# An attention-and-scan kernel: two score tiles of three PSUM banks, each of which may lend its third bank to VectorE

## The chip, the cores and the metric

The kernel runs on one core of a Trainium2 chip. The metric is the device time of one execution in microseconds (us). Four compute engines matter here: TensorE (PE in the profile; PEld is its weight load), VectorE (DVE), ScalarE (ACT) and GpSimd (POOL); SP issues most DMAs. PSUM, where TensorE puts its results, is used as eight banks of 128 partitions x 512 float32.

## The reference

Two independent halves are computed from separate inputs and laid side by side in the output. Half A is a diagonal state-space layer over 2048 steps and 640 channels; half B is attention with 32 query heads of 20 numbers, one shared key and one shared value head, without a mask:

```python
# A: Bu = x @ B_bar.T (complex);  h[t] = Lam_bar * h[t-1] + Bu[t];  y = 2*Re(h @ C.T) + x*Dskip
# B:
q = (x @ wq).reshape(B, S, 32, 20).transpose(0, 2, 1, 3)
k = x @ wk
v = x @ wv
scores = einsum("bhqd,bkd->bhqk", q, k) * (20 ** -0.5)
o = einsum("bhqk,bkd->bhqd", softmax(scores), v)
out_B = o.transpose(0, 2, 1, 3).reshape(B, S, 640) @ wo
out = concatenate([y, out_B], axis=-1)          # (1, 2048, 1280), bfloat16
```

## The kernel before

**Attention.** The 32 heads and 2048 queries make 32 groups `g`: a block of 512 queries by four heads. A group has 64 *units*, one for each of four heads `j` and 16 blocks `kc` of 128 keys. A unit is one matmul of scores (keys by queries, 128x512, one PSUM bank), an exponential, and the multiplication of the exponential with the values, which adds into the bank `PV`. There are 2048 units in all. The four heads lie in four 32-row strips of the array, so that up to four units are multiplied by one *fill* (`fill_op`), a burst of matmuls that TensorE works off side by side.

**Two ways to an exponential.** Most units take ACT: `ex_op` (line 1263) reads a whole *score tile* from PSUM, `R[0]` or `R[1]` in turn, and writes bfloat16 exponentials to `P`. The others, called *D units* here, take DVE: `dx_op` (line 1269) reads one bank and makes an integer whose bits are an approximate power of two, and three cheap shifted copies (`sh_op`, line 1274) are made from it in SBUF; four matmuls with the values then take the place of one, so that the errors average out. `raw_op` (line 1307) copies a finished group out of `PV`.

**PSUM before.** `R[0]` has three banks, `R[1]` has two (`TILES = (3, 2)`), `PV` has one and `B` has two (`BANKS = 2`). A bank of `B` is taken, used and given back, either by one D unit or by a piece of background work; `owner` says who has it. `R[0]` may *lend* its third bank, keyed `R0c`, to a D unit: the fill is then two banks for ACT and one for DVE (`size, d, x = 2, True, 2`).

**Background work** runs in threads beside the attention: `sa` (the inputs of the scan: five matmuls into a bank, then the product of line 901), `su` and `sr` (POOL's products around the scan, whose lines are 917 and 928), `sy` (half A's output, line 962), `qt`/`qd_block` (queries of the next block), `proj` (the output projection of half B, line 1061), `norm` and `dense` (the division by the softmax's denominators). Each matmul chain of `sa`, `sy`, `qt` or `proj` locks one bank with its first matmul and frees it with the DVE instruction that reads the result.

**The order of everything** is found while the program is built. `main` keeps a clock for each engine and, at each step, collects the candidates (a fill, an exponential, a shift, a group of PV matmuls, the head of each thread), gives each the time at which it could begin plus a bias, and emits the earliest. `want_d` decides whether a fill takes a D unit along: not if DVE's backlog is over a threshold, not if no bank is free soon enough (`spared`), and not if a background thread has waited too long for a bank (`starved`). The thresholds are drawn at random by `vary`; `SEEDS` holds one seed for each of 64 stretches of the 2048 units. `pv_op` takes exponentials from `items`, `P` is a ring of ten tiles (`PTILES`), 25 units in all, and an exponential waits while its tile's last content is still unread (`tile_left`). The end is `last_ops`: the projection of the last query block, in banks of `R`, `B` and `PV` (lines 1094 to 1104).

Of the kernel before, what the change touches and what calls it, by code (L numbers as in the profile page):

```python
# [217 lines left out]
def act_t(n):  # L218
    return n / 1200.0 + 0.05
# [24 lines left out]
class _Kernel:  # L244
    S, D, H, DH = 2048, 640, 32, 20
    NC, NQB, NKC, NGG = 5, 4, 16, 8
    BANKS = 2
    PIECES = "abcd"
    TILES, PTILES, DUNITS, DSHIFT, QRING = (3, 2), 10, 9, 3, 4
    SHIFTS = (0, 33, 65, 95)  # L250

# [13 lines left out]
    SEEDS = (19006, 20002, 21006, 22006, 23001, 24003, 25001, 26002, 27008, 28003, 0, 30006, 31008, 32005, 33006,  # L265
# [28 lines left out]
    def alloc(self):  # L294
        S, NC = self.S, self.NC
        nc = self.nc
        self.R = [self.scope.enter_context(nc.psum_tensor(f"R{i}", [128, 512 * n], FP32))
                  for i, n in enumerate(self.TILES)]
        self.PV = self.scope.enter_context(nc.psum_tensor("PV", [128, 512], FP32))
        self.BB = self.scope.enter_context(nc.psum_tensor("B", [128, 512 * self.BANKS], FP32))  # L300
        self.B = [self.BB[:, 512 * i:512 * i + 512] for i in range(self.BANKS)] + [self.R[0][:, 1024:1536]]
        self.bkeys = [f"B{i}" for i in range(self.BANKS)] + ["R0c"]
        self.p.psum.update(["R0", "R0c", "R1", "R1b", "PV", *(f"B{i}" for i in range(self.BANKS))])
# [25 lines left out]
        self.sb("P", [128, self.PTILES * 5 // 2, 512], BF16)  # L329
# [7 lines left out]
        self.wq_raw = self.P[:].rearrange("p s n -> p (s n)")[:, 18 * 512:18 * 512 + NC * 640].rearrange("p (c n) -> p c n", c=NC)  # L337
# [92 lines left out]
    def setup(self):  # L430
# [51 lines left out]
        pk = ["P7", "P8", "P9"]  # L482
# [23 lines left out]
        banks = [(K.R[1], 0, "R1"), (K.R[1], 512, "R1b"), (K.BB, 0, "B0"), (K.BB, 512, "B1")]  # L506
# [39 lines left out]
        for m, src, keys in ((0, K.R[1][:, 0:1024], ["R1", "R1b"]), (1, K.BB[:, 0:1024], ["B0", "B1"])):  # L546
# [342 lines left out]
    def scan_in(self, ops, dve, b, c):  # L889
        K, NC, prog = self, self.NC, self.prog  # L890
        u = NC * b + c
        xs = [f"xaT{b % 2}_{i}" for i in range(NC)]
        gate = lambda: prog["u"] >= u and prog["x"] >= b
        for k, (nm, BT) in enumerate((("BTre", K.BTre), ("BTim", K.BTim))):
            h = Hold()
            for cd in range(NC):
                ops.append(self.mms([self.m1(lambda h=h: h.T[:, :], BT[:, cd, 128 * c:128 * c + 128],
                                             K.xaT[:, b % 2, cd, :], cd == 0, cd == NC - 1)],
                                    [f"{nm}{i}" for i in range(NC)] + xs, [None], accum=cd > 0, lock=cd == 0,
                                    gate=gate if cd == 0 else None, hold=h))  # L900
            dve(lambda e, k=k, h=h: e.tensor_tensor(  # L901
                K.tm[:, 2 * k:2 * k + 2, :], bass.AP(tensor=K.BB, offset=512 * int(h.key[1]),
                                                       ap=[[512 * self.BANKS, 128], [0, 2], [1, 512]]),
                K.cs[:, c, :, :], ALU.mult), [None, "cosT", "sinT"], [f"tm{2 * k}", f"tm{2 * k + 1}"], 1024, hold=h,
                free=True, done=(lambda: prog.update(a=u + 1)) if k else None)
# [162 lines left out]
    def last_ops(self, gates, normed):  # L1068

        K, NC = self, self.NC  # L1070
        spots = [(K.R[0], 0, 0, 512, self.TILES[0]), (K.R[1], 1, 0, 512, self.TILES[1]), (K.BB, 2, 0, 512, self.BANKS)]
        keys = [["R0"], ["R1"], ["B0", "B1"], ["R0c", "PV"]]
# [40 lines left out]
    def vary(self, seed):  # L1113

        r = self.rng = random.Random(seed)
        self.backlog = r.choice((2.5, 3.0, 3.5, 4.0, 5.0))
        self.spared = r.choice(((0.02, 0.02, 0.02), (0.05, 0.15, 0.02), (0.1, 0.3, 0.02), (0.02, 0.3, 0.02)))
        self.after = r.choice((0.1, 0.15, 0.2)), r.choice((0.35, 0.4, 0.5))
        self.few, self.wait, self.noise = r.choice((1, 1, 2)), r.choice((0.15, 0.25, 0.35)), r.choice((0.0, 0.05, 0.1))

        self.starved = dict(sy=r.choice((0.0, 1.0, 4.0, 99.0)), sa=r.choice((2.0, 99.0)),
                            proj=r.choice((0.0, 1.0, 4.0, 99.0)),
                            qt=r.choice((0.0, 1.0, 4.0, 99.0)))
        self.lend = r.choice((0.5, 1.0))
        self.open, self.first = r.choice((0.6, 0.7)), r.choice(("sy", "proj", None))

    def main(self):
# [10 lines left out]
        tile_left = {}  # L1138
# [27 lines left out]
        fins = self.last_ops([lambda: done(0), lambda: done(1), lambda: done() and cur["raw"] == NG and not (any(owner[:2]) or sy or norm or proj),  # L1166
# [3 lines left out]
        owner = ["rest", "rest", None]  # L1170
        rest[-1].done = lambda: owner.__setitem__(slice(0, 2), [None, None])
        holds, since = {}, {}
# [57 lines left out]
        def want_d(g, t, n_tile, lent=False):  # L1230
# [9 lines left out]
            if any(owner[:2]) and any(t - x > self.starved[name] * (name != "qt" or len(self.qsent) > 0) for name, x in since.items()):  # L1240
                return False
            return (backlog(t) <= self.backlog - 0.5 * n_tile
                    and p.begin("pe", (), (f"B{bank(None)}",)) <= t + self.spared[n_tile])

        def fill_op(n, out, d, x):
            lst, reads, writes = [], set(), ([f"R{n % 2}"] if out else []) + ["R0c"] * (len(out) == 3)
# [13 lines left out]
        def ex_op(n, size):  # L1260
            b = 5 * (n // 2 % (self.PTILES // 2)) + 3 * (n % 2)
            dst = K.P[:, b:b + size, :].rearrange("p a n -> p (a n)")
            return Op("act", lambda e: e.activation(dst, K.R[n % 2][:, 0:512 * size], ACT.Exp, scale=self.exp_scale),  # L1263
                      [f"R{n % 2}"] + ["R0c"] * (size == 3), [f"P{n % self.PTILES}"], occ=act_t(512 * size), lat=0.17)
# [20 lines left out]
        def pv_op(g):  # L1285
            lst, keys = [], set()
            for j in range(4):
# [3 lines left out]
                if how == "act":  # L1291
                    rhs, w = K.P[:, b, :], 0
                    keys |= {f"P{a}", "VP0"}
# [18 lines left out]
        while True:  # L1312
# [33 lines left out]
            full = bool(tiles) and tile_left.get(tiles[0][0] - self.PTILES, 0) > 0  # L1346
            if tiles:
                n, out = tiles[0]
                if tile_left.get(n - self.PTILES, 0) == 0:
                    offer("ex", ex_op(n, len(out)), 0.0)  # L1350
# [19 lines left out]
            for name, th in threads:  # L1370
# [50 lines left out]
            if kind == "bg":  # L1421
                th = dict(threads)[name]
                th.popleft()
                if o.lock:
                    owner[int(o.hold.key[1])] = name
                    since.pop(name, None)
                if o.free:
# [3 lines left out]
            elif kind == "fill":  # L1431
                out, d, x = arg
                self.units += len(out) + (d is not None)
                if out:
                    n = cur["fill"]
                    cur["fill"] += 1
                    tile_left[n] = len(out)
# [12 lines left out]
            elif kind == "ex":  # L1450
                n, out = tiles.popleft()
                cur["act"] += 1
                b = 5 * (n // 2 % (self.PTILES // 2)) + 3 * (n % 2)
                for i, (g, j, kc) in enumerate(out):
                    items[g][j].append(("act", kc, n % self.PTILES, b + i, n))
# [17 lines left out]
            elif kind == "pv":  # L1473
                g = cur["pv"]
                for j in range(4):
                    if items[g][j]:
# [3 lines left out]
                        if how == "act":  # L1480
                            tile_left[h] -= 1
# [49 lines left out]
```

## Time and profile before

| | |
|---|---|
| time, median of 3 runs | 770.23 us (769.33 to 770.93) |
| the profiled execution | 770.28 us, of which the span of the trace is 768.6 us |
| busy: ACT / DVE / PE / POOL | 752.5 / 708.3 / 704.8 / 446.0 us |
| exponentials on ACT | 677 instructions: 258 of three banks, 419 of two (1612 units) |
| D units on DVE | 436: 363 through `B`, 73 through the lent bank of `R[0]` |
| granted TensorE clock, mean | 0.989 |

In the profile's groups a row gives the line, the engine, the operation, the tiles (output <- inputs, with buffer numbers left out, so `R` is either score tile), the shapes, the count, and behind the bar the time during which at least one such instruction ran and the mean duration in ns; behind the second bar stands the engine's idle time before them, and who ended it. Matmuls overlap one another, and so do ACT's instructions: their spacing is shorter than their duration. All matmuls bear one line, 421, of the helper that emits them.

### The profile page before, as it was taken

To read this page: it belongs to the slowest core of one execution; us is meant where nothing else is said; L and a number is where in the kernel's file an instruction comes from. 1 tells how busy PE (TensorE), PEld (TensorE's weight loads), DVE (VectorE), ACT (ScalarE), POOL (GpSimd) and SP (SyncE) were. 2 spreads that over 40 slices of the span, in tenths; PEclk is the share of its full clock that TensorE was granted. 3 is DMA by queue.
4 is the path that set the end of the run, shared out by engine and by line. 5 is a ranking of instruction groups with operands and counts; after the bars stand their busy time and mean duration, and the time that the engine had idled before them with its cause. 6 is when DMAs were issued, how large, how long until landed. Compare 5 with 4: busy or idle time off the path is not lost.

```text
span 768.6 us, 16664 instructions
## 1 busy us (share of the span) xinstructions
PE 704.8 (92%) x6538; PEld 213.4 (28%) x6538; DVE 708.3 (92%) x1236; ACT 752.5 (98%) x710; POOL 446.0 (58%) x867
## 2 busy tenths in 40 slices
PE   5799988888889999998889999988889999889998
PEld 2222222222222333322223323322223332223333
DVE  5599999999998999999997999999999789999986
ACT  8999999999999999999999999999999999999995
POOL 5612354579989931088997300199986469990040
PEclk9899999899999999999999999999999999999999
DMA  9366301000021100220002100040000201000020
GB/s 186 57 143 134 74 16 49 8 24 14 3 51 30 42 8 27 56 60 15 15 9 67 42 23 9 23 93 10 15 15 28 66 33 34 14 15 17 18 61 35
DMA packets 61179, 31.50 MB, mean 41 GB/s; under 512 B 41510, under 2 KB 61102, under 8 KB 61102
## 3 DMA queue, kind: packets, MB, share of 16 engines
q1 hardware_dynamic: 59606, 30.14, 15.9%
q8 instruction: 52, 0.85, 0.5%
q10 hardware_dynamic: 1496, 0.30, 0.2%
q14 instruction: 25, 0.20, 0.1%
HBM read 9.21 MB, written 12.69 MB: 28 GB/s over the span
## 4 chain that ended last, share of the span: by engine, by line
ACT 74%; PE 15%; DVE 9%; POOL 1%; DMA 1%; issue 1%; ACTq 0%; DVEq 0%; POOLq 0%
ACT P L1263 72%; PE R L421 5%; PE PV L421 5%; PE B L421 4%; DVE Pd L1274 4%; DVE Pd L1269 3%; DVE hh L928 1%; DVE tm L901 1%; POOL tm L858 1%; DMA WO<-in_B_wk_dram 1%; ACT cs L691 1%; ACT Pd L690 0%; ACT KT L538 0%; DVE CGre L860 0%; ACT L503 0%
## 5 line engine op out<-in xcount | busy, mean ns | idle before, releaser
L1263 ACT ACTIVATE P<-R 128x1024 bf16<-128x1024 f32 (+1 forms) x677 | 733.1, 1354 | 4.3 <-PE R L421 1.8
L421 PE MATMUL R<-QT,KT 32*128 32x512 bf16 (+1 forms) x1685 | 266.9, 389 | 48.6 <-ACT P L1263 37.1
L1269 DVE TENSOR_SCALAR Pd<-B 128x512 int16<-128x512 f32 x363 | 245.5, 682 | 19.4 <-PE B L421 17.0
L1274 DVE TENSOR_SCALAR Pd<-Pd 128x1536 int16<-128x1536 int16 (+2 forms) x513 | 260.2, 541 | 0.4
L421 PE MATMUL PV<-Pd,VP 128*32 128x512 bf16 x1744 | 256.9, 386 | 2.0 <-DVE OTr L1307 1.0
L421 PE MATMUL PV<-P,VP 128*32 128x512 bf16 x1612 | 253.3, 389 | 0.7 <-DVE OTr L1307 0.6
L917 POOL TENSOR_TENSOR tm<-hh,cs 128x128 bf16<-128x128 f32 x320 | 163.9, 533 | 17.7 <-DVE hh L928 8.3
L421 PEld LDWEIGHTS R<-QT,KT 32*128 32x128 bf16 (+1 forms) x1685 | 66.1, 91 | 301.0 <-ACT P L1263 271.0
L421 PE MATMUL B<-QT,KT 32*128 32x512 bf16 x363 | 141.0, 389 | 0.0
L917 POOL TENSOR_TENSOR uh<-tm 128x128 bf16<-128x128 bf16 x160 | 81.0, 527 | 97.6 <-DVE tm L901 93.7
L917 POOL TENSOR_TENSOR W<-tm 128x128 bf16<-128x128 bf16 x160 | 93.5, 608 | 49.4 <-PE B L421 45.3
L421 PEld LDWEIGHTS PV<-Pd,VP 128*32 128x32 bf16 x1744 | 60.1, 94 | 65.7 <-issue 40.5
L421 PEld LDWEIGHTS PV<-P,VP 128*32 128x32 bf16 x1612 | 58.1, 94 | 58.8 <-issue 46.6
L1011 POOL TENSOR_TENSOR OTd<-OTd,rwide 128x128 bf16<-128x128 bf16 x80 | 33.2, 443 | 60.0 <-DMA OTd<-o_rows 58.2
L1269 DVE TENSOR_SCALAR Pd<-R 128x512 int16<-128x512 f32 x73 | 49.9, 683 | 3.0 <-PE R L421 2.4
L901 DVE TENSOR_TENSOR tm<-B,cs 128x1024 bf16<-128x1024 f32 x40 | 48.5, 1213 | 1.0 <-PE B L421 0.6
L858 POOL TENSOR_SCALAR tm<-W,sc 128x128 f32<-128x128 bf16 x40 | 32.3, 821 | 27.5 <-DVE CGre L860 15.9
L421 PE MATMUL B<-CGre,W 128*128 128x384 bf16 (+1 forms) x160 | 46.4, 305 | 0.0
L421 PE MATMUL B<-CGim,W 128*128 128x384 bf16 (+1 forms) x160 | 45.5, 299 | 0.0
L928 DVE TENSOR_TENSOR_SCAN hh<-sc,hini,uh 128x512 f32<-128x512 f32 x30 | 40.7, 1358 | 0.0
L421 PEld LDWEIGHTS B<-QT,KT 32*128 32x128 bf16 x363 | 32.9, 91 | 0.0
L421 PE MATMUL B<-xaT,BTre 128*128 128x512 bf16 x100 | 30.1, 384 | 0.1
(149 smaller groups left out, 437.2 us busy)
## 6 DMA issues: line engine op xcount, KB each, us to landing
o_rows<-OTr SPq DMA_DIRECT2D x32, 128.0 KB, 1.7
QT<-q_rows SPq DMA_DIRECT2D x30, 128.0 KB, 2.2
q_rows<-Qd SPq DMA_DIRECT2D x16, 160.0 KB, 2.9
OTd<-o_rows SPq DMA_DIRECT2D x16, 160.0 KB, 3.4
out_dram<-ystage SPq DMA_DIRECT2D x16, 160.0 KB, 1.9
out_dram<-ostage SPq DMA_DIRECT2D x12, 160.0 KB, 1.8
P<-in_B_wq_dram SPq DMA_DIRECT2D x1, 800.0 KB, 5.6
WO<-in_B_wo_dram SPq DMA_DIRECT2D x4, 200.0 KB, 3.4
```

Of the source, the lines that this page charges most:

```text
L421: ins = e.matmul(o() if callable(o) else o, lhsT=l, rhs=r, start=st, stop=sp, skip_group_check=True, **kw)
L691: act(lambda e, c=c, b=b: e.activation(K.cs[:, c, :, :].rearrange("p i n -> p (i n)"), K.tri[:, 4 * b + 2:4 * b + 4, :].rearrange("p r n - ...
L858: pool(lambda e, y=y, c=c, gy=gy, i=i: e.tensor_scalar(K.ctmp[:, i:i + 128], y[:, i:i + 128], sc[:, gy, c:c + 1], None, op0=ALU.mult), key ...
L901: dve(lambda e, k=k, h=h: e.tensor_tensor(K.tm[:, 2 * k:2 * k + 2, :], bass.AP(tensor=K.BB, offset=512 * int(h.key[1]), ap=[[512 * self.BA ...
L917: put(lambda e, c0=c0, end=end: e.tensor_tensor(out[:, c0:end], a[:, c0:end], b[:, c0:end], op), reads, [writes + h], n, gate=None if i el ...
L928: dve(lambda e, ri=ri, ini=ini: e.tensor_tensor_scan(K.hh[:, ri, :], dec, K.uh[:, ri, :], ini, ALU.mult, ALU.add), ["sc", *(f"uh{ri}{h}" f ...
L1011: ops.append(Op("pool", lambda e, c=c, m=m: e.tensor_tensor(K.OTd[:, m, c], K.OTd[:, m, c], K.rwide[:, c], ALU.mult), rw + [f"OTe{dd}" for ...
L1263: return Op("act", lambda e: e.activation(dst, K.R[n % 2][:, 0:512 * size], ACT.Exp, scale=self.exp_scale), [f"R{n % 2}"] + ["R0c"] * (siz ...
L1269: return Op("dve", lambda e: e.tensor_scalar(K.Pd[:, 0, u, :], K.B[x][:, :], self.d_off, 0.0, op0=ALU.add, op1=ALU.max), [key], [f"Pd{u}_0 ...
L1274: return Op("dve", lambda e: e.tensor_scalar(K.Pd[:, i, a:b, :], K.Pd[:, 0, a:b, :], float(self.SHIFTS[i]), 0.0, op0=ALU.subtract, op1=ALU ...
```

## The change

`R[1]` gets a third bank, taken from `B`, which keeps one. Either tile may lend its third bank. The PSUM tensor `R1` now spans four banks: the tile's three and then the one that is left, `B0`. Background chains and D units of the old kind share `B0` alone; `bank()` returns 0 or nothing. The tile of a fill is two wide while its third bank is owned by a D unit, whether that is of this fill or of an earlier one.

`P` is a ring of 25 single units in place of ten tiles. An exponential is put where the last one ended, or at 0 where it would not fit, and waits until each of its slots has been read (`pleft`, `vacant`).

`vary` draws more: `lend` may also be 0.0 (how much less backlog a lent bank asks for), `prefer` lets a lent bank go ahead of `B0`, and `gap` holds a thread's next chain back for 0, 4 or 8 us after its last. The 64 seeds are new. In the setup, the banks that hold the keys' projection are renamed, and so are the last projection's.

The diff, cut to its core:

```diff
-    BANKS = 2
-    TILES, PTILES, DUNITS, DSHIFT, QRING = (3, 2), 10, 9, 3, 4
+    TILE, PUNITS, DUNITS, DSHIFT, QRING = 3, 25, 9, 3, 4
+    PWQ = 18
...
-    SEEDS = (19006, 20002, 21006, 22006, 23001, 24003, ...
+    SEEDS = (14003, 0, 16003, 17002, 18007, 19002, 20006, ...
...
-        self.B = [self.BB[:, 512 * i:512 * i + 512] for i in range(self.BANKS)] + [self.R[0][:, 1024:1536]]
-        self.bkeys = [f"B{i}" for i in range(self.BANKS)] + ["R0c"]
+        self.RB = self.scope.enter_context(nc.psum_tensor("R1", [128, 512 * (self.TILE + 1)], FP32))
+        self.R = [self.R0, self.RB[:, 0:512 * self.TILE]]
+        self.B = [self.RB[:, 1536:2048], self.R[0][:, 1024:1536], self.R[1][:, 1024:1536]]
+        self.bkeys = ["B0", "R0c", "R1c"]
...
-        self.lend = r.choice((0.5, 1.0))
+        self.lend, self.prefer = r.choice((0.0, 0.5, 1.0)), r.choice((False, True))
+        self.gap = dict(sy=r.choice((0.0, 4.0, 8.0)), proj=r.choice((0.0, 4.0, 8.0)), sa=r.choice((0.0, 0.0, 4.0)),
+                        qt=r.choice((0.0, 0.0, 4.0)))
...
+        def slot(size):
+            return room[0] if room[0] + size <= self.PUNITS else 0
+
+        def vacant(size):
+            b = slot(size)
+            return not any(pleft[b:b + size]) and not (rest and b + size > self.PWQ)
...
-            f = [i for i in range(2) if owner[i] is None]
-            if not f:
-                return None
-            return min(f, key=lambda i: p.begin("pe", (), (f"B{i}",)))
+            return 0 if owner[0] is None else None
...
             if lent:
-                return (self.lend < 9 and owner[2] is None and t_left() and backlog(t) <= self.backlog - 0.5 * n_tile - self.lend
-                        and p.begin("pe", (), ("R0c",)) <= t + self.spared[n_tile])
+                return (owner[lent] is None and t_left() and backlog(t) <= self.backlog - 0.5 * n_tile - self.lend
+                        and p.begin("pe", (), (self.bkeys[lent],)) <= t + self.spared[n_tile])
...
-                    size, x = self.TILES[n % 2] - (n % 2 == 0 and owner[2] is not None), bank(None)
+                    lent = 1 + n % 2
+                    size, x = self.TILE - (owner[lent] is not None), bank(None)
                     d = want_d(g, t, n % 2)
-                    if not d and size == 3 and want_d(g, t, 0, True):
-                        size, d, x = 2, True, 2
+                    if (not d or self.prefer) and size == 3 and want_d(g, t, 0, lent):
+                        size, d, x = 2, True, lent
...
+                    if o.lock and t_left() and not (name == "qt" and not self.qsent):
+                        bias += max(0.0, last.get(name, -99.0) + self.gap.get(name, 0.0) - p.clock["pe"])
```

More of the change, by code (lines that the diff above doesn't have):

```diff
@@ L296, in alloc @@
         nc = self.nc
-        self.R = [self.scope.enter_context(nc.psum_tensor(f"R{i}", [128, 512 * n], FP32))
-                  for i, n in enumerate(self.TILES)]
+        self.R0 = self.scope.enter_context(nc.psum_tensor("R0", [128, 512 * self.TILE], FP32))
         self.PV = self.scope.enter_context(nc.psum_tensor("PV", [128, 512], FP32))
-        self.BB = self.scope.enter_context(nc.psum_tensor("B", [128, 512 * self.BANKS], FP32))
-        self.B = [self.BB[:, 512 * i:512 * i + 512] for i in range(self.BANKS)] + [self.R[0][:, 1024:1536]]
-        self.bkeys = [f"B{i}" for i in range(self.BANKS)] + ["R0c"]
-        self.p.psum.update(["R0", "R0c", "R1", "R1b", "PV", *(f"B{i}" for i in range(self.BANKS))])
+        self.RB = self.scope.enter_context(nc.psum_tensor("R1", [128, 512 * (self.TILE + 1)], FP32))
+        self.R = [self.R0, self.RB[:, 0:512 * self.TILE]]
+        self.B = [self.RB[:, 1536:2048], self.R[0][:, 1024:1536], self.R[1][:, 1024:1536]]
+        self.bkeys = ["B0", "R0c", "R1c"]
+        self.p.psum.update(["R0", "R0c", "R1", "R1b", "R1c", "PV", "B0"])
         self.sb("xbT", [128, NC, S], BF16)
@@ L328, in alloc @@
         self.sb("ident", [128, 128], BF16)
-        self.sb("P", [128, self.PTILES * 5 // 2, 512], BF16)
+        self.sb("P", [128, self.PUNITS, 512], BF16)
         self.sb("Pd", [128, 4, self.DUNITS, 512], I16)
@@ L481, in setup @@
                 ["wk_raw", "wk4"], ["wk4"], n=100)
-        pk = ["P7", "P8", "P9"]
+        pk = [f"P{u}" for u in range(self.PWQ, self.PUNITS)]
         go(self.dma(K.wq_raw, t["wq"].rearrange("(c p) n -> p c n", p=128), "wq", writes=["wq_raw"] + pk, kb=800))
@@ L503, in setup @@
         act(lambda e: e.activation(K.half[:, 2:3], K.half_pi[:], ACT.Exp), ["half_pi", "half"], ["half2"], n=1)
-        banks = [(K.R[1], 0, "R1"), (K.R[1], 512, "R1b"), (K.BB, 0, "B0"), (K.BB, 512, "B1")]
+        banks = [(K.RB, 0, "R1"), (K.RB, 512, "R1b"), (K.RB, 1024, "R1c"), (K.RB, 1536, "B0")]
         for bt, off, key in banks:
@@ L544, in copy @@
                         occ=dve_t(512))
-        for m, src, keys in ((0, K.R[1][:, 0:1024], ["R1", "R1b"]), (1, K.BB[:, 0:1024], ["B0", "B1"])):
+        for m, src, keys in ((0, K.RB[:, 0:1024], ["R1", "R1b"]), (1, K.RB[:, 1024:2048], ["R1c", "B0"])):
             dve(lambda e, m=m, src=src: e.tensor_reduce(
@@ L1070, in last_ops @@
         K, NC = self, self.NC
-        spots = [(K.R[0], 0, 0, 512, self.TILES[0]), (K.R[1], 1, 0, 512, self.TILES[1]), (K.BB, 2, 0, 512, self.BANKS)]
-        keys = [["R0"], ["R1"], ["B0", "B1"], ["R0c", "PV"]]
+        spots = [(K.R0, 0, 0, 512, 3), (K.RB, 1, 0, 512, 4), (K.RB, 2, 1024, 1536, 4)]
+        keys = [["R0"], ["R1"], ["R1c", "B0"], ["R0c", "PV"]]
         banks = [[T[:, a:a + 320], T[:, b:b + 320]] for T, _, a, b, _ in spots] + [[K.R[0][:, 1024:1344], K.PV[:, 0:320]]]
@@ L1137, in main @@
         begun = [[False] * 4 for _ in range(NG)]
-        tile_left = {}
         dunit_left = {}
@@ L1165, in main @@
         done = lambda k=None: all(x == 64 for x in taken) and not any(k in (None, n % 2) for n, _ in tiles)
-        fins = self.last_ops([lambda: done(0), lambda: done(1), lambda: done() and cur["raw"] == NG and not (any(owner[:2]) or sy or norm or proj),
+        fins = self.last_ops([lambda: done(0), lambda: done(1), lambda: done() and cur["raw"] == NG and not (any(owner) or sy or norm or proj),
                               lambda: done() and cur["raw"] == NG],
@@ L1169, in main @@
         threads = [("rest", rest), ("norm", norm), ("dense", dense), ("proj", proj), ("qt", qt), ("qr", qr), ("sy", sy), ("sa", sa), ("su", su), ("sr", sr), ("sc", sc_), ("sx", sx), *fins]
-        owner = ["rest", "rest", None]
-        rest[-1].done = lambda: owner.__setitem__(slice(0, 2), [None, None])
-        holds, since = {}, {}
+        owner = ["rest", None, "rest"]
+        rest[-1].done = lambda: owner.__setitem__(slice(0, 3, 2), [None, None])
+        pleft, room = [0] * self.PUNITS, [0]
+        def slot(size):
[3 more added lines that the diff above has]
+            return not any(pleft[b:b + size]) and not (rest and b + size > self.PWQ)
+        holds, since, last = {}, {}, {}
         def bank(o):
-            f = [i for i in range(2) if owner[i] is None]
-            if not f:
-                return None
-            return min(f, key=lambda i: p.begin("pe", (), (f"B{i}",)))
+            return 0 if owner[0] is None else None
         def made(g, j):
@@ L1228, in t_left, with want_d @@
             return taken[NG - 1] < 40
-        def want_d(g, t, n_tile, lent=False):
+        def want_d(g, t, n_tile, lent=0):
             if not (g > 0 or taken[g] >= 24) or d_group(g) is None:
@@ L1235, in want_d @@
             if lent:
-                return (self.lend < 9 and owner[2] is None and t_left() and backlog(t) <= self.backlog - 0.5 * n_tile - self.lend
-                        and p.begin("pe", (), ("R0c",)) <= t + self.spared[n_tile])
+                return (owner[lent] is None and t_left() and backlog(t) <= self.backlog - 0.5 * n_tile - self.lend
+                        and p.begin("pe", (), (self.bkeys[lent],)) <= t + self.spared[n_tile])
             if bank(None) is None:
                 return False
-            if any(owner[:2]) and any(t - x > self.starved[name] * (name != "qt" or len(self.qsent) > 0) for name, x in since.items()):
+            if any(t - x > self.starved[name] * (name != "qt" or len(self.qsent) > 0) for name, x in since.items()):
                 return False
@@ L1245, in fill_op @@
         def fill_op(n, out, d, x):
-            lst, reads, writes = [], set(), ([f"R{n % 2}"] if out else []) + ["R0c"] * (len(out) == 3)
+            lst, reads, writes = [], set(), ([f"R{n % 2}"] if out else []) + [f"R{n % 2}c"] * (len(out) == 3)
             units = list(out) + ([d] if d else [])
@@ L1260, in ex_op @@
         def ex_op(n, size):
-            b = 5 * (n // 2 % (self.PTILES // 2)) + 3 * (n % 2)
+            b = slot(size)
             dst = K.P[:, b:b + size, :].rearrange("p a n -> p (a n)")
             return Op("act", lambda e: e.activation(dst, K.R[n % 2][:, 0:512 * size], ACT.Exp, scale=self.exp_scale),
-                      [f"R{n % 2}"] + ["R0c"] * (size == 3), [f"P{n % self.PTILES}"], occ=act_t(512 * size), lat=0.17)
+                      [f"R{n % 2}"] + [f"R{n % 2}c"] * (size == 3), [f"P{b + i}" for i in range(size)], occ=act_t(512 * size), lat=0.17)
         def dx_op(n):
@@ L1292, in pv_op @@
                     rhs, w = K.P[:, b, :], 0
-                    keys |= {f"P{a}", "VP0"}
+                    keys |= {f"P{b}", "VP0"}
                 else:
@@ L1345, in main @@
                             offer("fill", fill_op(n, [], d, bank(None)), 0.2, arg=([], d, bank(None)))
-            full = bool(tiles) and tile_left.get(tiles[0][0] - self.PTILES, 0) > 0
+            full = bool(tiles) and not vacant(len(tiles[0][1]))
             if tiles:
                 n, out = tiles[0]
-                if tile_left.get(n - self.PTILES, 0) == 0:
+                if not full:
                     offer("ex", ex_op(n, len(out)), 0.0)
@@ L1426, in main @@
                     since.pop(name, None)
+                    last[name] = p.clock["pe"]
                 if o.free:
@@ L1436, in main @@
                     cur["fill"] += 1
-                    tile_left[n] = len(out)
                     tiles.append((n, [(g, j, left[g][j].pop()) for g, j in out]))
@@ L1452, in main @@
                 cur["act"] += 1
-                b = 5 * (n // 2 % (self.PTILES // 2)) + 3 * (n % 2)
+                b = slot(len(out))
+                room[0] = b + len(out)
+                pleft[b:room[0]] = [1] * len(out)
                 for i, (g, j, kc) in enumerate(out):
-                    items[g][j].append(("act", kc, n % self.PTILES, b + i, n))
+                    items[g][j].append(("act", kc, b, b + i, n))
             elif kind == "dx":
@@ L1480, in main @@
                         if how == "act":
-                            tile_left[h] -= 1
+                            pleft[b] = 0
                         else:
```

9 lines of the change are left out of this document (5 added, 4 removed), and 8 rows, old and new, of the table SEEDS.

## The prediction

> **What bounds the kernel now.** I read the page's shares and the chain first. The profiled execution took 770.28 us, 1.7 more than its span and as good as the median (770.23), so sums are made on 770.3.
>
> ```profile
> PE 704.8 (92%) x6538; PEld 213.4 (28%) x6538; DVE 708.3 (92%) x1236; ACT 752.5 (98%) x710; POOL 446.0 (58%) x867
> ...
> ACT 74%; PE 15%; DVE 9%; POOL 1%; DMA 1%; issue 1%; ACTq 0%; DVEq 0%; POOLq 0%
> ```
>
> ACT is busy 98% of the span and is three quarters of the chain that ended last; DVE and PE stand close behind. The groups by form say what ACT does, and the timeline of ACT how closely.
>
> ```profile
> L1263 ACT ACTIVATE P<-R 128x1024 bf16<-128x1024 f32 x419 | 457.8, 1189 | 1.1 <-PE R L421 0.7 <-PE B L421 0.2
> L1263 ACT ACTIVATE P<-R 128x1536 bf16<-128x1536 f32 x258 | 418.3, 1621 | 3.2 <-PE R L421 1.2 <-PE B L421 1.1 <-PE PV L421 0.6
> L1269 DVE TENSOR_SCALAR Pd<-B 128x512 int16<-128x512 f32 x363 | 245.5, 682 | 19.4 <-PE B L421 17.0
> L1269 DVE TENSOR_SCALAR Pd<-R 128x512 int16<-128x512 f32 x73 | 49.9, 683 | 3.0 <-PE R L421 2.4
> ```
>
> ```profile
> 319.82 1.61 ACT L1263 ACTIVATE P<-R 128x1536 bf16<-128x1536 f32 x1
> ...
> 321.15 1.19 ACT L1263 ACTIVATE P<-R 128x1024 bf16<-128x1024 f32 x1
> ...
> 322.06 1.21 ACT L1263 ACTIVATE P<-R 128x1024 bf16<-128x1024 f32 x1
> ```
>
> An exponential of three banks starts 1.33 us ahead of the next, one of two 0.91; over all 677 the medians of the spacing are 1331 and 904 ns. So a bank costs 1331 - 904 = 427 ns and an instruction 904 - 2 x 427 = 50 ns besides. From the first exponential (21.7 us) to the end of the last (759.0) pass 737.4 us: 1612 units x 427 = 688.3, 677 x 50 = 33.9, and 15.2 in which the spacing is longer. The last 15.2 are stalls, 12.4 of them behind two-bank exponentials.
>
> The windows show where the other engines bind:
>
> ```profile
> core 0: us, PE busy (x) PEld busy (x) DVE busy (x) ACT busy (x) POOL busy (x), PEclk, DMA share, GB/s
> ...
> 320.00:400.00 80.00, 71.08 (x669) 20.46 (x671) 78.49 (x128) 79.62 (x74) 66.97 (x130) 1.00 0.13 34
> 400.00:480.00 80.00, 79.47 (x727) 25.09 (x720) 71.55 (x128) 79.93 (x75) 24.88 (x54) 1.00 0.12 34
> 480.00:560.00 80.00, 71.62 (x673) 20.07 (x671) 77.23 (x128) 79.72 (x75) 58.54 (x113) 1.00 0.15 37
> 560.00:640.00 80.00, 76.83 (x722) 25.23 (x719) 71.87 (x123) 79.55 (x74) 55.60 (x115) 1.00 0.12 34
> ```
>
> They alternate: where half A's output and the projections crowd PE (79.5 of 80), DVE runs dry (8.4 us idle); elsewhere DVE is full and PE has 9 us to spare. ACT is full throughout. So the time can move in three ways: fewer instructions on ACT, fewer stalls, or a unit more or less on DVE.
>
> **The change part by part.**
>
> *How many exponentials.* Each tile has three banks; it is two wide when a D unit sits in the third. With L lent units and x tiles whose third bank is still held by an older one, the count is (1612 + L + x) / 3. L depends on how many D units still find `B0`. I paired, in the trace, the first matmul of each background chain with the end of the DVE instruction that reads it: 40 chains of `sa` hold a bank 139.6 us, 32 of `sy` 107.2, the query blocks 90.6, 28 of `proj` 55.9; 393 us in all, and two at once for 14 us only. One bank carries that, and leaves 737 - 393 = 344 us. A D unit holds a bank 1.47 us on average (median 1.29, one in ten over 2.14). Of the 365 us in which one chain held one bank, the other had a D unit for 179 (49%); of the 380 us without a chain, some D unit sat in `B` for 288 (76%). So `B0` takes 344 x 0.49 / 1.47 = 115 to 344 x 0.76 / 1.47 = 178 D units; I take 145, nearer to the first row, which is that of a single free bank. Then L = 436 - 145 = 291. For x: a tile is refilled two exponentials later, 1.81 to 2.66 us, against the hold above; some 5% of the lent banks come too late, 15 (0 to 40). The count is 1918 / 3 = 639, 38 fewer: 38 x 50 ns = **-1.9 us** (-2.6 with 178 and 5, -1.0 with 115 and 40).
>
> The Trainium skill ("ScalarE: Activation LUTs", section "What ACT_TABLE_LOAD costs") gives an ACTIVATE 186 or 280 ns of fixed cost and an overlap of 93 ns between neighbours, so 93 to 187 ns an instruction; by that this term would be -3.5 to -7.1 us. The trace has its 0.83 ns a column but 50 ns for the rest, and the measured spacing decides.
>
> *PE.* Every one of the 677 fills serves a tile; no D unit of before has a fill of its own. From a fill's first matmul to the next work of PE pass 323 ns (median over the fills), so 38 fewer fills give PE 12 us, about 4 of them in the crowded windows. That, and fewer two-bank exponentials, behind which the stalls lie, take an estimated **-1.0 us** off the 15.2. The bounds are -4 (a quarter of the stalls gone) and +4 (a lent tile's fill must wait for DVE too: the 73 of before had PE wait 3.2 us for line 1269 in all, and four times as many would make that 13, of which ACT sees a third).
>
> *D units.* One costs DVE (245.5 + 49.9 + 260.2) / 436 = 1.27 us and saves ACT 427 ns plus a third of 50. If DVE's idle time falls by i, both engines end together with i / (1.27 + 0.44) units more and the time falls by 0.26 i. Between 22 and 745 us DVE idles 43 us, 21 of these waiting for a fill with a D unit. Lending now works at every fill, and chains and D units no longer compete for most of it; against that stands one bank less for all. I take i = 4, **-1.0 us**; bounds 15 less idle (most of that in the three crowded windows), -3.9, and 25 more, +6.5.
>
> *At nothing:* the ring by slot holds the same 25 units, and the profile shows no exponential waiting for its place (0.6 us behind PV); were the cover gone, a stall is one PV group, 0.3 us. The reads of a lent bank cost the same as of `B` (683 and 682 ns). The renamed banks of setup leave the instructions before 21.7 us as they are. The 9.6 us after the last exponential keep their operations.
>
> Sum: 770.3 - 1.9 - 1.0 - 1.0 = **766.4 us**. The likeliest case's own range runs from 760 to 769.
>
> **The rivals.**
>
> *DVE goes short (slower).* The mechanism: a fill takes a D unit only if its bank is free within 0.02 to 0.3 us. While a chain holds `B0` (half the time, over 70% in the crowded windows, where chains held 57 of 80 us), the one other place is this tile's third bank, and where the former D unit is still in it, the fill is two wide and brings DVE nothing. For it speaks that DVE already waits 17.0 us for fills of `B`, with two banks. Against it: the lent bank is free at nine refills in ten. The price: 400 to 480 us shows 8.4 us idle in 80; were all like that, idle rises by 25 and the time by 6.5, less 1.9: 774.9. It decides from 11 us more idle (nine D units fewer), where it eats the first two terms. Chance 0.24.
>
> *The change does little.* If lent banks are used at nearly every fill and `B0` almost never (50 D units), the count is (1612 + 386 + 15) / 3 = 671, saving 0.3 us; PE and DVE gain nothing: 770. For it speaks `prefer`; against it, that `B0` is asked first otherwise. Chance 0.13.
>
> *A later end (slower).* Lending stops at the last group's 40th unit; then D units, half B's last chains and the last division share one bank. Four chains of `proj` at 2.0 us each, in a row in place of in pairs, would cost up to 4: 770.3 - 1.9 + 4 = 772.4. The timeline has DVE's last shifts end at 758.6, with ACT's last exponential, so nothing is slack there. Chance 0.04.
>
> *The clock.* With 12 us less work PE might be granted less. From 20 to 40 us it got 0.83 and ACT was busy 18.7 of 20; two more such stretches add 2.6, for 771.0. Against it: PE idles 9 us of 80 in three windows at a granted 1.00. Chance 0.02. The Trainium skill ("TensorE: Matmul & The Clock Gate", section "HAM oscillation — how this bites in real kernels") warns of gaps over some 3.4 us; the longest in this trace after 25 us is 0.96 us.
>
> **How the numbers follow.** The forecast has 0.57. A difference of 0.2% (1.5 us) is about what a measurement of this kernel can tell from no change. Faster by more: 0.57; within it 0.13; slower 0.24 + 0.04 + 0.02 = 0.30. The range: below, -2.6 - 3.9 - 4 in full gives 759.8, so 760; above, it takes in the first slower case at its price, 775. I leave out a tenth at each end.
>
> **What would show it.** Exponentials between 626 and 658, over half of them three wide at 1331 ns; lines 1269 with `Pd<-R` some 260 to 320 times; D units (a quarter of the `PV<-Pd` matmuls) 430 to 450; DVE's idle time before line 1269 not above 20 us; PE's busy time down in the crowded windows. It is wrong if the D units fall under 427, if the count of exponentials stays over 665, or if the time from the last exponential to the end grows by over 1 us.

## The result: slower by 0.6%, and the profile after

The changed kernel takes 774.42 us in the median (773.02 to 775.15, 4 runs) beside 769.80 for the kernel before: a ratio of 1.0058, with a 95% interval of 1.0037 to 1.0079 (the kernel before has four runs by now). The forecast was 766.4. The loss of 4.6 us lies inside the range given, on the side that had a chance of 0.30. The profiled execution took 773.02, the fastest of the four; its span, 771.3 us, is 2.7 over that of before.

From the page after: the shares, and the chain by engine. Below it are the shares of a second profile of the same kernel, taken on another chip (the last run below).

```profile
PE 680.9 (88%) x6466; PEld 212.8 (28%) x6533; DVE 712.9 (92%) x1210; ACT 752.2 (98%) x700; POOL 438.7 (57%) x867
...
ACT 70%; DVE 17%; PE 11%; issue 1%; DMA 1%; ACTq 0%
```

```profile
PE 697.2 (90%) x6533; PEld 212.1 (27%) x6533; DVE 712.2 (92%) x1210; ACT 751.9 (97%) x700; POOL 437.1 (57%) x867
```

ACT is as busy as before and still bounds the kernel. The chain has changed hands behind it: DVE carries 17% in place of 9, PE 11 in place of 15. PE's 680.9 us is too low: the first profile has 6533 weight loads but only 6466 matmuls, so 67 matmul records are missing, none of them of a fill. The second lacks none and has PE busy 697.2 us. The groups by form (line 1271 is the exponential, 1277 the first conversion of a D unit; the second tile and `B0` are one tensor now, so all their rows read `R`):

```profile
L1271 ACT ACTIVATE P<-R 128x1536 bf16<-128x1536 f32 x277 | 409.3, 1605 | 4.2 <-PE R L422 2.6 <-issue 1.3
L1271 ACT ACTIVATE P<-R 128x1024 bf16<-128x1024 f32 x390 | 398.1, 1176 | 4.3 <-PE R L422 4.1
...
L1277 DVE TENSOR_SCALAR Pd<-R 128x512 int16<-128x512 f32 x437 | 292.8, 682 | 22.1 <-PE R L422 18.7
```

There are 667 exponentials in place of 677, and 437 D units in place of 436. In the order that the program writes, 369 of the 437 go through a lent bank and 68 through `B0`; 21 further tiles are two wide without lending. The spacing is still 1330 and 904 ns. Idle time ahead of exponentials has grown from 4.3 to 8.5 us.

From the first exponential (21.2 us) to the end of the last (762.6) pass 741.4 us, against 737.4. By the prediction's own split: 1611 units x 427 = 687.9 (-0.4), 667 x 50 = 33.4 (-0.5), and stalls, 20.1 (+4.9). The first exponential starts 0.5 earlier and the part after the last is 0.8 shorter (8.7 in place of 9.5). So -0.4 - 0.5 + 4.9 - 0.5 - 0.8 = +2.7, the difference of the spans: all of the loss is stalls.

The waits of PE's matmuls into `R`, first before, then after (engine, tile and line, who was waited for: us in total, times, longest). After, these rows hold the chains in `B0` too; of the 8.3 us, the fills alone wait 6.9, in 17 waits:

```profile
PE R L421 <- ACT P L1263: 37.1, 125, 1.2
PE R L421 <- DVE Pd L1269: 3.2, 8, 0.8
```

```profile
PE R L422 <- ACT P L1271: 49.1, 157, 1.2
PE R L422 <- DVE Pd L1277: 8.3, 22, 1.1
```

A fill that finds ACT still reading its tile costs nothing, ACT being busy. A fill that waits for DVE may starve ACT. The longest such case, from the timeline after (start, duration, what, and in brackets the idle time before and who ended it):

```profile
414.76 1.47 DVE L929 TENSOR_TENSOR_SCAN hh<-sc,hini,uh 128x512 f32<-128x512 f32 x1
...
416.15 0.53 DVE L963 CAST ystage<-R 128x384 bf16<-128x384 f32 x1
416.60 1.95 DVE L1277 TENSOR_SCALAR Pd<-R 128x512 int16<-128x512 f32 x3
417.39 0.13 PEld L422 LDWEIGHTS R<-QT,KT 32*128 32x128 bf16 x3 [1.57 <-ACT P L1271]
417.42 0.39 PE L422 MATMUL R<-QT,KT 32*128 32x512 bf16 x3 [1.10 <-DVE Pd L1277]
...
417.86 1.02 ACT L1271 ACTIVATE P<-R 128x1024 bf16<-128x1024 f32 x1 [0.69 <-PE R L422]
```

A scan of 1.47 us and a copy keep DVE; three conversions queue behind them. The fill at 417.42 goes to the tile whose third bank the first of them has yet to read. PE stands for 1.10 us, and ACT for 0.69.

I traced each stall of ACT over 60 ns to its fill, and to who ended PE's idle time around it. How far back one looks for other work moves the last two columns by some 1 us. Per profile, in us:

| | all over 60 ns | the fill waits for DVE | other work ahead of it waits for DVE | the rest: PE busy with other work |
|---|---|---|---|---|
| before | 11.9 | 1.1 | 3.0 | 7.8 |
| after | 18.0 | 6.1 | 4.7 | 7.2 |

### The profile page after: what moved, and what is told of

Its sections match the earlier page's. It is cut to its first block, busy times and chain, and to the rows that moved or that the text cites. A ratio compares the mean times of both kernels' runs of the same rounds, so it can differ in the third digit from the quotient of the medians.

```text
span 771.3 us, 16618 instructions
## 1 busy us (share of the span) xinstructions
PE 680.9 (88%) x6466; PEld 212.8 (28%) x6533; DVE 712.9 (92%) x1210; ACT 752.2 (98%) x700; POOL 438.7 (57%) x867
## 4 chain that ended last, share of the span: by engine, by line
ACT 70%; DVE 17%; PE 11%; issue 1%; DMA 1%; ACTq 0%
ACT P L1271 68%; PE R L422 7%; DVE Pd L1282 6%; DVE Pd L1277 5%; PE PV L422 4%; DVE hh L929 2%; DVE tm L902 2%; ACT cs L692 1%; DVE Qd L776 1%; DMA WO<-in_B_wk_dram 1%; ACT Pd L691 0%; ACT KT L539 0%; DVE OTr L1315 0%; DVE rblk L992 0%; DVE ostage L1062 0%
## 5 line engine op out<-in xcount | busy, mean ns | idle before, releaser
L1277 DVE TENSOR_SCALAR Pd<-R 128x512 int16<-128x512 f32 x437 | 292.8, 682 | 22.1 <-PE R L422 18.7
L422 PE MATMUL PV<-P,VP 128*32 128x512 bf16 x1611 | 247.2, 388 | 0.9 <-ACT P L1271 0.4
L918 POOL TENSOR_TENSOR W<-tm 128x128 bf16<-128x128 bf16 x160 | 88.7, 575 | 21.6 <-PE R L422 17.4
L902 DVE TENSOR_TENSOR tm<-R,cs 128x1024 bf16<-128x1024 f32 x40 | 48.5, 1213 | 0.3
L422 PE MATMUL R<-CGre,W 128*128 128x384 bf16 (+1 forms) x160 | 46.4, 305 | 0.1
L422 PE MATMUL R<-CGim,W 128*128 128x384 bf16 (+1 forms) x160 | 45.5, 299 | 0.0
L422 PE MATMUL R<-WO,OTd 128*128 128x320 bf16 x160 | 30.4, 302 | 1.4 <-DVE tm L902 1.1
L422 PE MATMUL R<-xaT,BTre 128*128 128x512 bf16 x85 | 26.0, 385 | 2.9 <-issue 1.3
L422 PE MATMUL R<-xbT,wqd 128*128 128x512 bf16 x87 | 26.7, 384 | 1.6 <-issue 1.4
L422 PE MATMUL R<-xaT,BTim 128*128 128x512 bf16 x84 | 25.6, 383 | 2.2 <-issue 1.4
```

The costliest lines, as they stand in the source:

```text
L422: ins = e.matmul(o() if callable(o) else o, lhsT=l, rhs=r, start=st, stop=sp, skip_group_check=True, **kw)
L902: dve(lambda e, k=k, h=h: e.tensor_tensor(K.tm[:, 2 * k:2 * k + 2, :], bass.AP(tensor=K.RB, offset=1536, ap=[[2048, 128], [0, 2], [1, 512] ...
L918: put(lambda e, c0=c0, end=end: e.tensor_tensor(out[:, c0:end], a[:, c0:end], b[:, c0:end], op), reads, [writes + h], n, gate=None if i el ...
L1277: return Op("dve", lambda e: e.tensor_scalar(K.Pd[:, 0, u, :], K.B[x][:, :], self.d_off, 0.0, op0=ALU.add, op1=ALU.max), [key], [f"Pd{u}_0 ...
```

## The experiments

Four theories. **A / D1**: the loss is fills that wait for DVE, since now nearly each D unit sits in a score tile. **B**: the new order has PE reach its fills late, whatever DVE does. **C**: the layout is sound, and its seeds are only less well searched. **D** holds the layout itself guilty, D2 by its one bank for chains.

**DVE early, the order kept.** In both kernels the first conversion of a D unit was narrowed, which leaves out three quarters of these units' scores; no instruction was moved:

```diff
-            return Op("dve", lambda e: e.tensor_scalar(K.Pd[:, 0, u, :], K.B[x][:, :], self.d_off, 0.0, op0=ALU.add,
+            w = 512 if n < self.DUNITS else 128
+            return Op("dve", lambda e: e.tensor_scalar(K.Pd[:, 0, u, 0:w], K.B[x][:, 0:w], self.d_off, 0.0, op0=ALU.add,
```

> The kernel before in its own order of instructions, with DVE's first conversion of a D unit (line 1269) cut from 512 to 128 columns after the first nine units; three quarters of those units' scores are left out. Each of 427 conversions falls from 0.68 to about 0.28 us, so DVE is early everywhere. Theory A (the loss of the change is fills that wait for DVE): the kernel before has few of these, about 1 us of ACT's stalls stand directly behind them and 3 us behind other work of PE that waits for DVE, so it gains 2 to 4 us: 766 to 768. Theory B (the loss is in the new order itself, PE reaching its fills late because other work is ahead of them): about the same here, since both say that DVE is not what mainly stalls this kernel.

> The same cut in the changed kernel, again in its own order, 428 conversions cut. Theory A: the 6 us of ACT's stalls behind fills that wait for DVE, and some of the 5 us behind other work that waits for DVE, go: 763 to 767, as fast as the kernel before with the same cut or up to 2 us faster (10 exponentials fewer are worth 0.5, the earlier end the rest). Theory B: the new order keeps its stalls, so it stays 3 to 5 us behind the kernel before with the same cut: 769 to 772.

Measured beside 768.62 for the kernel before on that chip: 768.99 with the narrow conversion (ratio 1.000, 0.9988 to 1.0011) and 768.16 for the changed kernel with it (0.9989, 0.9978 to 1.0000). So the cut brought the kernel before nothing, a miss of the 2 to 4 us that both theories granted it, though its profile has 2.1 us less stall. With it the changed kernel is level with the kernel before, where without it it is 0.6% behind (measured on two other chips). That is A's comparison, and B's, 3 to 5 us behind, did not come; the time itself lies between the two ranges, for the missed gain lifts both kernels. The groups and waits of the changed kernel with the cut:

```profile
L1278 DVE TENSOR_SCALAR Pd<-R 128x128 int16<-128x128 f32 x428 | 121.4, 287 | 123.2 <-PE R L422 118.8
```

```profile
PE R L422 <- ACT P L1271: 48.5, 163, 1.0
PE R L422 <- DVE Pd L1278: 0.4, 1, 0.4
```

Fills waited 6.9 us for conversions; now 0.4. Stalls fell from 19.6 to 13.7 (before: 14.8 to 12.7; here against the medians for each width), those behind fills that wait for DVE from 6.1 to 0.8. The spacing of the exponentials is still 1330 and 904 ns in both cut kernels, so ACT itself did not get faster. It shows that the loss of this order lies in DVE's lateness. It does not show why the order leaves so little room for it.

**The price of an instruction.**

```diff
...
+                if size == 3:
+                    e.activation(dst[:, 0:1024], K.R[n % 2][:, 0:1024], ACT.Exp, scale=self.exp_scale)
+                    return e.activation(dst[:, 1024:1536], K.R[n % 2][:, 1024:1536], ACT.Exp, scale=self.exp_scale)
...
```

> The kernel before, each of its 258 three-bank exponentials written as one of two banks and one of one bank, same order otherwise. It measures what one exponential more costs. By the spacing of the trace (904 ns for two banks, 427 a bank, so 50 an instruction) 258 x 50 = 12.9 us more, up to 3 of it hidden in stalls: 780 to 783. By 93 to 187 ns an instruction, the price worked out from the skill's page on ScalarE, 24 to 48 us more: 794 to 818.

784.25 us, 15.6 more, a little over the first range: 60 ns an instruction by the time, and 56 from the first to the last exponential (751.8 us against 737.4); after the last, 9.5 us pass in both. So 50 was a little low, but sound. The price of 93 to 187 ns, an estimate worked out from the Trainium skill ("ScalarE: Activation LUTs", section "What ACT_TABLE_LOAD costs"), does not hold for these back-to-back exponentials.

**The ring alone**, in the kernel before with its own seeds (`slot`, `vacant` and `pleft` as in the change's diff, 25 slots):

> One part of the change alone: the ring of 25 single slots for the exponentials, put into the kernel before with its tiles of three and two banks, its two banks for other work and its own seeds. The order that comes out has 681 exponentials, 434 D units (78 lent). Theory A: a slot costs nothing on the chip; 4 exponentials more are 0.2 us, 2 units more on ACT 0.9: about 771 if nothing else changes. Theory C (seeds found for one order are worth several us, and any change of the order without new seeds loses them): 773 to 778, with more stalls on ACT spread over the whole run.

774.99 us, ratio 1.0074 (1.0056 to 1.0093), as C has it: stalls 17.2 us, the part after the last exponential 11.4 in place of 9.5. The run alone would also fit a ring that costs time; with seeds of equal search (below) ring and draws together cost 0.7 us. So the loss here is most likely that of seeds found for another order. From here on all compared kernels have seeds of equal search.

**The layout at equal search.** `SEEDS` was replaced in the kernel before and in the changed one; a third kernel has ring and wider draws (`lend`, `prefer`, `gap`) with the tiles and banks of before.

> The kernel before with seeds found anew by one short search (for each of the 64 stretches in turn eight draws, the one kept whose finished order ends soonest by the kernel's own clocks); 683 exponentials, 427 D units, 79 of them lent. It is the reference for the next two, which have seeds of the same search. Any theory: its order is poorer than that of the long search behind the kernel before; 6 exponentials and 9 units more on ACT are 4.2 us, and more stalls: 773 to 780.

> The changed kernel, both tiles of three banks and one bank for other work, with seeds of the same short search; 663 exponentials, 435 D units, 344 lent. Theory D (the layout itself costs time: every chain and every unlent D unit shares one bank, and fills wait for DVE): over 5 us slower than the kernel before with seeds of the same search, with longer stalls on ACT, most behind fills that wait for DVE. Theory C (only the seeds of the change were less well searched): within 2 us of it, or 4 us faster, since 20 exponentials fewer are worth 1 us and 8 units fewer on ACT 3.4.

> The other parts of the change without its layout: ring by slot and the wider draws (lend from 0, prefer, gap) in the kernel before with its tiles of three and two banks and two banks for other work, seeds of the same short search; 684 exponentials, 427 D units, 83 lent. Theory D: as the kernel before with seeds of the same search, within 2 us. If ring or draws are what costs time, 4 us or more slower than it, whatever the layout.

779.16, 799.30 and 779.85 us, in the order of the three texts: the other parts cost 0.7, within the noise, and the layout 19.4 more, 20.1 in all. But 18.8 of these are one stall, and it does not stand behind a fill that waits for a conversion, as D expected of most. The timelines of ACT and PE around it:

```profile
70.65 3.28 ACT L1267 ACTIVATE P<-R 128x1024 bf16<-128x1024 f32 x3 [0.76 <-PE R L418]
92.62 1.94 ACT L1267 ACTIVATE P<-R 128x1024 bf16<-128x1024 f32 x2 [18.69 <-PE R L418]
```

```profile
75.66 1.25 PE L418 MATMUL R<-xbT,wqd 128*128 128x512 bf16 x5 [0.46 <-DVE Qd L772]
78.17 1.24 PE L418 MATMUL R<-xaT,BTre 128*128 128x512 bf16 x5 [1.26 <-issue]
80.73 0.61 PE L418 MATMUL R<-Qabs,Md 128*32 128x512 bf16 x2 [1.32 <-POOL tm L855]
81.52 0.39 PE L418 MATMUL R<-Qabs,Md 128*32 128x512 bf16 x1 [0.18 <-DVE Qabs L788]
84.46 0.79 PE L418 MATMUL R<-Qabs,Md 128*32 128x512 bf16 x2 [2.55 <-DVE Qabs L788]
```

The first block's queries (`wqd`, then `Md`) and the scan's inputs (`BTre`) take turns in one bank; the `Md` chain holds it from 80.7 to 86.0 us while its matmuls wait for DVE. The next scores need these queries, so ACT starves until 92.6. The changed kernel's own seeds avoid this. A second search of the same kind gave a cleaner pair:

> The changed kernel with seeds of a second short search (other draws, same effort); 660 exponentials, 431 D units, 336 lent. The first such search left it one stall of 18.8 us at 73 us. Theory D: 3 to 8 us slower than the kernel before with seeds of this second search, with the difference in ACT's stalls. Theory C: within 2 us of it or faster, as 22 exponentials fewer (1.1) and 7 units fewer on ACT (3.0) would have it.

> The kernel before with seeds of the second short search; 682 exponentials, 424 D units, 74 lent. Any theory: near the first such search, 779 (776 to 783).

780.59 and 778.97 us, beside 769.17 for the kernel before on that chip (1.0147, 1.0130 to 1.0164; 1.0126, 1.0098 to 1.0153). The intervals overlap: 1.6 us, under the 3 to 8 that D expected and within the 2 of C. The forms show both sides, the changed kernel first:

```profile
L1267 ACT ACTIVATE P<-R 128x1536 bf16<-128x1536 f32 x297 | 428.4, 1560 | 4.0 <-PE R L418 3.6
L1267 ACT ACTIVATE P<-R 128x1024 bf16<-128x1024 f32 x363 | 366.3, 1152 | 8.3 <-PE R L418 7.8
```

```profile
L1259 ACT ACTIVATE P<-R 128x1024 bf16<-128x1024 f32 x422 | 458.8, 1186 | 1.4 <-PE R L417 0.7 <-PE PV L417 0.5 <-PE B L417 0.2
L1259 ACT ACTIVATE P<-R 128x1536 bf16<-128x1536 f32 x260 | 418.7, 1610 | 6.8 <-PE R L417 3.4 <-PE B L417 3.0
```

| pair | instructions | units on ACT | stalls | sum | times |
|---|---|---|---|---|---|
| own seeds | 677 to 667: -0.5 | 1612 to 1611: -0.4 | 14.8 to 19.6: +4.8 | +3.9 | +4.6 |
| first short search | 683 to 663: -1.0 | 1621 to 1613: -3.4 | 18.6 to 43.2: +24.6 | +20.2 | +20.1 |
| second short search | 682 to 660: -1.1 | 1624 to 1617: -3.0 | 18.8 to 24.5: +5.7 | +1.6 | +1.6 |

Stalls are those of the profile and times the medians of all runs, and the sums leave out what lies before the first exponential and after the last, so an agreement to 0.1 is in part luck. In each pair the layout saves instructions and brings stalls, some 5 to 6 us of them even without the long one. Poorly searched, it also feeds DVE more D units, which pays for most of that. The long search had already brought the kernel before to 436 D units; that nothing was left there to pay with is likely, but not shown.

The stalls are not of one kind. With the own seeds, 4.1 of the 4.8 us come after the first 100 us of the trace. In the short searches 22.6 of the 24.6 us, and 3.2 of the 5.7, fall within these 100, in which the first queries and the inputs of the scan share the one bank. The fills' waits for conversions are 3.3 and 3.5 us in the first pair and 2.4 and 4.7 in the second (3.2 and 6.9 with the own seeds), while the third kernel, with the banks of before, has 4.6. So D1 is shown for the own seeds alone; at equal search it is at most a part. C is right that the price depends on the seeds. That the layout costs time at equal search is not clear of noise once the long stall is left out; the stalls speak for it. What a search of the changed kernel as long as that of before would give is open.

**The rule on the third bank mended.**

```diff
-                    size, x = self.TILE - (owner[lent] is not None), bank(None)
+                    size, x = self.TILE - (owner[lent] is not None or p.begin("pe", (), (self.bkeys[lent],)) > t + 0.05), bank(None)
...
-                    if (not d or self.prefer) and size == 3 and want_d(g, t, 0, lent):
+                    if not d and size == 3 and want_d(g, t, 0, lent):
```

> The changed kernel with its rule on the third bank mended: a tile is filled three wide only if DVE can have read the third bank's last D unit by then, by the kernel's own clocks (0.05 us of grace), and a lent bank no longer goes ahead of the one for other work. Seeds of the same short search as the two pairs' first; 686 exponentials, 425 D units, 349 lent. Theory D1 (what the layout costs is fills that wait for DVE): few such waits are left, and it comes within 3 us of the kernel before with seeds of that search (779): 777 to 782. Theory D2 (it costs by the one bank for other work): no better than the changed kernel with seeds of that search without its one long early stall: 781 or more, with chains late.

777.98 us (ratio 1.0117, 1.0098 to 1.0136), level with the kernel before at the same search, and within D1's range; D2's 781 or more did not come. Stalls are back at 19.1. But fills still wait for conversions, with ACT idle behind them:

```profile
PE R L418 <- DVE Pd L1273: 5.2, 14, 0.6
```

```profile
258.27 0.39 PE L418 MATMUL R<-QT,KT 32*128 32x512 bf16 x3 [0.65 <-DVE Pd L1273]
...
258.71 1.02 ACT L1267 ACTIVATE P<-R 128x1024 bf16<-128x1024 f32 x1 [0.35 <-PE R L418]
```

Of these 5.2 us the fills alone wait 4.8, in 12 waits; with seeds of the same search and the old rule they wait 3.5, in 12 too. So the time came as D1 forecast, without the waits going as it wants. The long stall is gone, but seeds and two lines of the rule changed at once, and what removed it is not shown. The reason for the layout is gone too, as tiles go two wide rather than wait:

```profile
L1267 ACT ACTIVATE P<-R 128x1024 bf16<-128x1024 f32 x435 | 434.6, 1190 | 5.6 <-PE R L418 5.4
L1267 ACT ACTIVATE P<-R 128x1536 bf16<-128x1536 f32 x251 | 369.5, 1620 | 2.2 <-PE R L418 1.5 <-PE PV L418 0.5
```

That is 686 exponentials, more than the layout of before needs with seeds of that search (683): the third banks that are not waited for are left out.

**Again, on another chip.**

> The changed kernel as it is, beside the kernel before on the same chip, to see whether the loss is there on another chip. 0.4 to 0.8% slower by every theory; within 0.2% if the first measurement was of its chip.

773.82 us beside 769.17, 1.0058 (1.0040 to 1.0075): the loss is the kernel's. Its profile splits the stalls into 4.0 behind fills that wait for DVE, 5.0 behind other such work and 8.8 of the rest, so the first two together, 9.0, are again twice the 4.1 of before.

## Why the prediction was wrong, by its own steps

**How many exponentials** (-1.9 forecast, -0.5 measured). The bound of ACT and 50 ns an instruction held. What failed is `B0`'s share: 145 D units forecast, 115 at least, and 68 came. The chains hold the bank 401 us, near the 393 forecast, and the 327 us between the first chain and the last fall into 123 gaps. 73 of these are under 1.5 us, about one hold of a D unit, but they make only 44 us; 202 us lie in 18 gaps of 4 us or more, in which 146 conversions start and only 54 of them read `B0`. So the room was there, and the program did not use it. By the order that it writes, 156 of the 369 lent units were lent while a chain held `B0`. But 100 were lent while `B0` was free and kept for a chain that had waited long enough (`starved`), 66 while its last content would not be read in time, and 34 because `prefer` put the lent bank first (the last 13 for other reasons). The forecast took the shares of the kernel before, and gave `prefer` and the waiting chains no term. Thus 369 lent units, not 291, each a third of an instruction; x was 21 where 15 was forecast. (The 380 us without a chain, from which the upper share was taken, count the setup; within the 737 us they are 357.)

**PE** (-1.0 forecast, +4.9 measured). This is the step with the wrong sign, and the whole of the loss. The relief is there, though smaller than the 12 us of the forecast: in the profile that lacks no record PE is busy 697.2 us in place of 704.8, and the crowded stretch from 400 to 480 us has PE at 77 of 80:

```profile
400.00:480.00 80.00, 76.98 (x732) 25.33 (x729) 74.59 (x124) 78.78 (x74) 45.19 (x99) 0.99 0.16 42
```

ACT did not get it: it idles 1.2 us there, where before it idled 0.1. The mechanism that cost the time stood in the text as the upper bound, "a lent tile's fill must wait for DVE too", priced at 13 us of waits of which ACT sees a third. The fills' waits were 6.9, and the stalls behind such fills and behind other work that waits for DVE grew by 6.7, from 4.1 to 10.8. It should have been the middle of the term: with five times as many lent units, waits for DVE were likely to grow, and DVE, idle for 43 of 723 us before, had little slack to be on time. That DVE's lateness is the loss, the narrowed conversions show.

**D units** (-1.0 forecast, -0.4 measured). Between 22 and 745 us DVE's idle time fell from 43 to 36 us, more than the 4 forecast; over the whole span it fell by 1.9 only (60.3 to 58.4), and 0.26 x 1.9 = 0.5 is about what came, one D unit more. But this input was chosen with the result known; with the stretch that the forecast used, the rule would give four units more. So the rule is not confirmed, and why only one came is open.

**At nothing**: setup and the end were to stay; they gained 0.5 and 0.8.

**The rivals.** "DVE goes short" had the sign and its chance of 0.24, with another mechanism: DVE got its units, and it was ACT that waited for DVE. It was to be told by fewer than 427 D units, and there are 437. (By the prediction's own rule its 11 us of idle time would have been six units, not nine.) The later end did not come, nor did the clock: 0.993 granted in place of 0.989. PE's longest idle time after 25 us in the trace of before is 1.23 us, not 0.96, at 26 us; the granted clock fell to half for 3.4 us at 120 us and for 6.8 at 141 all the same. "The change does little" had the count nearly right, 671, and named `prefer`, one of the reasons. Of the signs listed as refuting, the count over 665 came true.

The medians differ by 4.6 and the profiles by 2.7; the changed kernel's runs spread more (773.0 to 775.2), and the profiled one was the fastest. What varies between them stays open.

## What to carry to other kernels

Two engines that read banks of one tile are coupled through the next fill of that tile: the fill comes when the later of them has finished. Lend a bank of the bounding engine's tile only to an engine that has slack, and price the waits first, the saved instructions second. Where an order was searched for, compare layouts at equal search, and more than one search: here a single one would have shown 20 us, one stall's worth, where another showed 1.6.

## What was not expected of the hardware

An exponential more costs 56 to 60 ns here when the neighbours stand back to back (258 more cost 15.6 us). With 427 conversions of 0.29 us in place of 0.68, DVE's busy time in the kernel before fell from 708.3 us, 92% of the span, to 563.7, and none of it showed in the time.
